# Recurrent retention and a squared-ReLU feed-forward on one core: the second token block's output product done as seven half-size products, with another order around it

## The chip, the core and the metric

The kernel runs on one core of a Trainium2 chip. The core has engines that work side by side, each through its own queue, strictly in order: TensorE (PE in the profile; its weight loads are PEld) for matrix products, VectorE (DVE), ScalarE (ACT), GpSimd (POOL), and SyncE (SP), which issues most transfers. Products land in PSUM, eight banks of 2 KB per partition; everything else works on SBUF. Engines wait for one another through semaphores. The metric is device time in microseconds (us); lower is better.

## What is computed

```
state = gamma * state + outer(k_t, v_t);  y_t = scale * q_t @ state     # 4 batches, 8 heads, 768 steps, head size 64
x = y as 3072 tokens x 512
out = relu(x @ w_in)**2 @ w_out                                         # 512 -> 2048 -> 512
```

The recurrence is computed in chunks of 128 tokens: masked scores within a chunk and a running state between chunks, with the decay put into scaled copies of q and k. There are 24 chunks.

## The kernel before

**Blocks.** The 24 chunks are cut into 11 token blocks (BLOCKS): the first has four chunks, the others two. For a block the feed-forward first computes h = relu(x @ w_in) squared (the *first product*, `first_product`, L848: four matmuls for each of 16 slices of 128 hidden features), with ScalarE taking the relu out of PSUM (L857) and the square done on VectorE (L828) or, for a few, on ScalarE (L826). The *second product* multiplies h by w_out.

**Seven products.** For a 256-token block the second product, cut into two by two halves, can be done as seven products of half size instead of eight, with sums of halves of h (s1 to s4, made per block on VectorE), sums of halves of w_out (t1 to t4, `sum_w_out`, made once) and sums of the results (u, v, and the two output tiles). `seven_products` does this for the blocks in SEVEN, which are 2 to 10 (L28); `last_of_first` does it for half of block 0, whose other half is done plainly (`plain(j)`, L1036, eight steps, each of four matmuls of 512 columns and one of 256). Block 1 does the second product plainly: 32 matmuls of 512 columns (L1174). The last of the seven products of a block is kept back (`kept`) and runs in the next block's first product.

**The order.** Everything is put in order by hand. Blocks yield after each piece, a counter n rises by one for each, and `before(n)` runs whatever was `put` at that place. Block 0's pieces end at place 32, block 1's are places 33 to 48, block 2's begin after 48. `attend(m, ...)` places the steps of chunks 4 to 7: scaling q and k, turning q and k on TensorE through the one PSUM bank "tp" (pool `ps_tp`, one buffer; `transpose_q` L408, `transpose_k` L421), copying the turned k into the tile k_bd by two ScalarE instructions (L428), scores into the one bank "st" (L447) with a mask on VectorE (L454), `state` (L475/L486, copied out to s_bd), and `outputs` into the bank "y" (L515, L523, copied to xt on ScalarE, L531). Later chunks (`attend2`) turn q and k by transfers. In `seven_products` the accumulator pa is a tile of that same bank "tp"; pb, pe and pd are of the four-buffer pool "psf".

**Tiles.** The pool "h2" has three buffers of 4096 elements per partition: at the start `spare`, then the two of block 0, then one for each block in turn. s1, s2 and s4 of blocks 2 to 10 are kept in the tiles k_bds[0], k_bds[1] and v_bds[0], which chunks 4 to 7 use before that.

**Transfers.** SyncE issues q, k, v and w_in; GpSimd issues w_out, four parts of 512 KB that are cast on the way (`load_w_out`, L185, places 6, 8, 11, 14). GpSimd also casts v, zeroes the two k_big tiles and makes constants (`pack_constants`). VectorE zeroes the unused halves of seven other tiles (`zero_off_diagonal`, L375, places 35 on). `keep_awake` (L359) issues idle matmuls early on, while the inputs are on their way.

Of the kernel before, what the change touches and what calls it, by code (L numbers as in the profile page):

```python
# [9 lines left out]
FP32 = mybir.dt.float32  # L10
# [4 lines left out]
ALU = mybir.AluOpType  # L15
# [9 lines left out]
PACK_FROM = 8  # L25


SEVEN = range(2, 11)  # L28


@with_exitstack
def kernel(
# [163 lines left out]
        load_w_in(g)  # L196


    lng = const.tile([P, H], FP32)
    for h in range(H):  # L200
        nc.gpsimd.memset(lng[:, h : h + 1], float(np.log(gammas[h])))
# [125 lines left out]
    HN = DM // 2  # L327
    sums = [const.tile([P, NFB // 2, HN], BF16, name=f"w_sum{i}") for i in range(4)]

    def sum_w_out(half):  # L330

        src = w_out_halves[half].rearrange("s (j k) (n c) -> s k n j c", k=2, n=2)
        (b11, b12), (b21, b22) = ([src[:, k, n] for n in range(2)] for k in range(2))
        t1, t2, t3, t4 = (t[:, 4 * half : 4 * half + 4] for t in sums)
        for out, in0, in1 in ((t1, b12, b11), (t2, b22, t1), (t3, b22, b12), (t4, b21, t2)):
            yield nc.vector.tensor_tensor(out=out, in0=in0, in1=in1, op=ALU.subtract)

    def cast_w(kind, g, halves=(0, 1), on="VVSG"):

# [11 lines left out]

    idle_ps = []

    def keep_awake(n, width=4 * C, pool=ps_f, name="psf"):
        if not idle_ps:
            idle_ps.append(pool.tile([P, 4, P], FP32, name=name))
        wide = max(1, width // C)
        for _ in range(n):
            nc.tensor.matmul(  # L359
                idle_ps[0][:, 0:wide, 0 : width // wide],  # L360
                lhsT=ident[:],
                rhs=ident[:, None, 0 : width // wide].to_broadcast([P, wide, width // wide]),
                start=True,
                stop=True,
            )

    def end_awake():
        idle_ps.clear()
# [3 lines left out]
    xts = {}  # L372

    def zero_off_diagonal(t, hh):
        nc.vector.memset(t[halves[hh], :, 1 - hh, :], 0.0)  # L375

    def scale(engine, out, by, table):
        engine.tensor_tensor(  # L378
# [483 lines left out]
    def seven_products(tb):  # L862
# [4 lines left out]
            t.rearrange("s p hh d -> s (p hh d)").rearrange("s (j t) -> s j t", t=C)  # L867
            for t in (k_bds[0], k_bds[1], v_bds[0])
        )
        s3 = a21  # L870
        t1, t2, t3, t4 = sums
        b11, b21, b22 = (
# [108 lines left out]
    def last_of_first():  # L981
# [34 lines left out]
            add(s1[x], a21[x], a22[x])  # L1016
            add(s2[x], s1[x], a11[x], ALU.subtract)

        def last_sums():
            for x in range(2):  # L1020
                add(s3[x], a11[x], a21[x], ALU.subtract)
            for x in range(2):
                add(s4[x], a12[x], s2[x], ALU.subtract)

        def second_products():
            ops = [ps_f.tile([P, DM], FP32, name="psf") for _ in range(2)]
            pa, pe, pd, pb = (
                t[:, n * HN : (n + 1) * HN]
                for t in [ps_f.tile([P, DM], FP32, name="psf") for _ in range(2)]
                for n in range(2)  # L1030
            )
            oa, ob = (opool.tile([P, DM], FP32, name="osb") for _ in range(2))
            a, u, v = (upool.tile([P, HN], FP32, name=f"u{i}") for i in range(3))
            r0 = 2 * C

            def plain(j):  # L1036
                for f in (2 * j, 2 * j + 1):
                    for c, op in enumerate(ops):
                        nc.tensor.matmul(  # L1039
                            op[:],  # L1040
                            lhsT=h_of(0, f)[:, 0, c * C : (c + 1) * C],
                            rhs=w_out_bf[f // FPQ][:, f % FPQ, :],
                            start=(f == 0),
                            stop=(f == NFB - 1),
                        )
# [17 lines left out]
            nc.scalar.activation(a[:], pa, AF.Copy)  # L1063
# [5 lines left out]
            product(pa, a12, b(1, 0), lo, False)  # L1069
            product(pa, a12, b(1, 0), hi, False)  # L1070
            nc.scalar.activation(oa[:, 0:HN], pa, AF.Copy)
            yield
            product(pd, s1, t1, hi)
            yield
            product(pb, s2, t2, hi)
            add(u[:], pb, a[:])
            yield
            product(pe, a22, t4, hi)
            yield
            product(pb, s3, t3, lo, False)  # L1080
            yield
            product(pb, s3, t3, hi, False)
            add(v[:], pb, a[:])
            add(ob[:, HN:DM], pd, v[:])
            add(ob[:, 0:HN], pe, v[:])

            def last_product():
                product(pd, s4, b(1, 1), range(8), False)
                add(oa[:, HN:DM], pd, u[:])
                yield  # L1090
                nc.sync.dma_start(out[r0 + C : r0 + 2 * C], ob[:])
                yield
                nc.sync.dma_start(out[r0 : r0 + C], oa[:])
                yield

            kept.append(last_product())
            yield

        return first_sums, last_sums, second_products

    open_ps = {}

    def first_unit(tb, g, c, parts=(0, 1)):
# [98 lines left out]
    spare = hpool.tile([P, 4096], BF16, name="h2")  # L1202
    keep_awake(7, pool=ps_y, name="y")
    scale_q4(0, 0)
    scale_q4(0, 1)
    transpose_q4(0, 0, *tp)
# [85 lines left out]
    def attend2(m, d, before, q_at, qturn_at, k_at, turn_at, v_at):  # L1292
# [107 lines left out]
```

## Time and profile before

| | us |
|---|---|
| median of 3 runs (lowest, highest) | 204.95 (204.93, 205.1) |
| the profiled execution's own time | 205.18 |
| its span, first to last instruction | 203.0 |
| PE busy in the span | 195.8 (96%) |
| DVE / ACT / POOL busy | 150.0 / 127.5 / 75.4 |

The profiled execution took 2.18 us more than its span, and is 0.23 us over the median. The granted TensorE clock was 0.999 over the span. Times in the profile's views are counted from the span's start. In the timeline view the columns are start, duration, engine, line, what was done, and in brackets how long the engine had been idle before and for what. A matmul's duration there is its way through the array; the distance between starts is what it costs TensorE. In the chain views the columns are start, length, engine, bank and line.

### The profile page before, as it was taken

The numbers are of one execution on the slowest core, as the hardware profiler recorded it, in microseconds if no ns is written. First come the engines' busy times: TensorE is split into PE (matmuls) and PEld (weight loads), VectorE is DVE, ScalarE is ACT, GpSimd is POOL, SyncE is SP. The second block draws the span as 40 slices with busy tenths as digits, with TensorE's granted clock in tenths as the row PEclk, the third lists the DMA queues.
The fourth block names the chain that finished last, engine by engine and source line by source line (L and its number), as shares of the span: only waits on it lengthen the run. The fifth ranks groups of instructions, "written<-read, shape, count | busy, mean of one in ns | idle before, by whom it ended". The sixth has DMA issues, their size and how long they took to land.

```text
span 203.0 us, 5812 instructions
## 1 busy us (share of the span) xinstructions
PE 195.8 (96%) x2351; PEld 163.3 (80%) x2351; DVE 150.0 (74%) x322; ACT 127.5 (63%) x258; POOL 75.4 (37%) x143
## 2 busy tenths in 40 slices
PE   5989999999999999999999999999999999999993
PEld 1558545669975998999999999999899999999883
DVE  3786898898797679677787777777787787485374
ACT  8764873455744676693794784774785775763730
POOL 8683721087220873461722084323382022100000
PEclk9999999999999999999999999999999999999999
DMA  5999999999798798979999479999999856200202
GB/s 167 356 374 397 321 198 196 243 232 251 226 203 200 190 141 131 200 180 251 145 215 197 140 130 187 175 227 199 166 133 195 155 107 53 103 3 0 107 0 105
DMA packets 92250, 36.55 MB, mean 180 GB/s; under 512 B 68544, under 2 KB 88256, under 8 KB 92224
## 3 DMA queue, kind: packets, MB, share of 16 engines
q1 hardware_dynamic: 77312, 32.52, 67.8%
q0 software_dynamic: 14912, 3.67, 19.2%
q8 instruction: 18, 0.29, 0.6%
q14 instruction: 8, 0.07, 0.1%
HBM read 27.26 MB, written 6.29 MB: 165 GB/s over the span
## 4 chain that ended last, share of the span: by engine, by line
PE 93%; DVE 2%; DMA 2%; issue 1%; ACT 1%; DVEq 0%
PE psf L848 42%; PE psf L882 18%; PE tp L882 7%; PE psf L1039 3%; PE psf L1174 3%; PE psf L1006 3%; DMA qn<-in_q_dram 2%; PE y L805 2%; PE st L749 2%; PE y L798 2%; PE c_ps L776 2%; PE c_ps L644 1%; PE y L359 1%; PE y L523 1%; PE st L447 1%
## 5 line engine op out<-in xcount | busy, mean ns | idle before, releaser
L848 PE MATMUL psf<-xt,w_in_bf 128*128 128x256 bf16 (+2 forms) x880 | 92.3, 259 | 0.2 <-issue 0.2
L848 PEld LDWEIGHTS <-w_in_bf 128*128 128x128 bf16 x880 | 71.2, 98 | 11.4 <-issue 0.2
L857 ACT ACTIVATE h<-psf 128x512 bf16<-128x512 f32 x96 | 56.1, 595 | 21.3 <-PE psf L848 19.0
L828 DVE TENSOR_TENSOR h<-h 128x512 bf16<-128x512 bf16 x80 | 33.6, 432 | 21.6 <-ACT h L857 21.2
L727 POOL COPY v_bd<-v 64x512 bf16<-64x512 bf16 x32 | 21.6, 675 | 75.0 <-DVE v L719 70.9
L882 PEld LDWEIGHTS <-h 128*128 128x128 bf16 x288 | 26.5, 98 | 3.0 <-DVE h L828 0.3
L160 POOL DMA_DIRECT2D k_big<-in_k_dram x32 | 21.1, 675 | 0.0
L882 PE MATMUL psf<-w_sum,h 128*128 128x256 bf16 x136 | 19.1, 273 | 0.0
L882 PE MATMUL tp<-w_out_bf,h 128*128 128x256 bf16 x136 | 19.1, 273 | 0.0
L882 PE MATMUL psf<-w_sum,k_bd 128*128 128x256 bf16 x144 | 17.9, 273 | 0.0
L878 DVE TENSOR_TENSOR u<-psf,u 128x256 f32<-128x256 f32 x18 | 7.6, 424 | 11.2 <-PE psf L882 10.8
L882 PEld LDWEIGHTS <-k_bd 128*128 128x128 bf16 x144 | 13.8, 98 | 1.5
L785 ACT ACTIVATE s_bd<-c_ps 64x256 bf16<-64x256 f32 x29 | 10.7, 370 | 6.5 <-PE c_ps L776 6.5
L878 DVE TENSOR_TENSOR osb<-psf,u 128x256 f32<-128x256 f32 x26 | 10.3, 421 | 6.1 <-PE psf L882 5.8
L378 DVE TENSOR_TENSOR qs<-qn,qf 128x512 bf16<-128x512 f32 x20 | 14.2, 713 | 0.0
L786 ACT ACTIVATE s_bd<-c_ps 64x256 bf16<-64x256 f32 x29 | 11.0, 379 | 0.4
L756 DVE TENSOR_TENSOR pt<-st,cmask 128x512 bf16<-128x512 f32 x16 | 11.0, 688 | 0.1
L719 DVE TENSOR_TENSOR v<-stage,kf 128x512 bf16<-128x512 f32 x16 | 11.0, 685 | 0.0
L812 ACT ACTIVATE xt<-y 128x512 bf16<-128x512 f32 x16 | 9.6, 599 | 1.8 <-PE y L805 1.2
L918 ACT ACTIVATE osb<-tp 128x256 f32<-128x256 f32 x8 | 3.1, 385 | 12.2 <-PE tp L882 12.2
L826 ACT ACTIVATE h<-h 128x512 bf16<-128x512 bf16 x16 | 10.1, 630 | 0.5
L878 DVE TENSOR_TENSOR k_bd<-h 128x512 bf16<-128x512 bf16 x18 | 10.1, 559 | 0.3
(149 smaller groups left out, 296.1 us busy)
## 6 DMA issues: line engine op xcount, KB each, us to landing
qn<-in_q_dram SPq DMA_DIRECT2D x12, 512.0 KB, 5.5
out_dram<-osb SPq DMA_DIRECT2D x23, 256.0 KB, 2.6
stage<-in_v_dram SPq DMA_DIRECT2D x32, 96.0 KB, 4.1
stage<-in_moe_w_in_dram SPq DMA_DIRECT2D x4, 512.0 KB, 7.2
stage<-in_moe_w_in_dram SPq DMA_DIRECT2D x2, 1024.0 KB, 8.4
w_out_bf<-in_moe_w_out_dram POOLq DMA_DIRECT2D x4, 512.0 KB, 10.1
kn<-in_k_dram SPq DMA_DIRECT2D x6, 256.0 KB, 6.3
k_big<-in_k_dram POOLq DMA_DIRECT2D x32, 48.0 KB, 3.8
```

Of the source, the lines that this page charges most:

```text
L160: nc.gpsimd.dma_start(t[rows, :, p, hh, :], k[b, 2 * p + hh, (i + 3 * n) * C : (i + 3 * n + 3) * C].rearrange("(w s) d -> s w d", s=64),)
L378: engine.tensor_tensor(out=out, in0=by, in1=table[:, :, None].to_broadcast([P, H, D]), op=ALU.mult)
L719: nc.vector.tensor_tensor(out=v2.rearrange("s (u p) d -> s u p d", u=2), in0=vn, in1=kf2[:, i, :, :, None].to_broadcast([P, 2, NPAIR, D]), ...
L727: nc.gpsimd.tensor_copy(v_bd[rows, :, hh, :], v2[rows])
L756: nc.vector.tensor_tensor(out=pt[:], in0=st[:], in1=cmask2.rearrange("s r t -> s (r t)")[:, None, :].to_broadcast([P, 2 * NPAIR, C // 2]), ...
L785: nc.scalar.activation(s_bd[halves[0], :, 0, :], c[halves[0]], AF.Copy)
L786: nc.scalar.activation(s_bd[halves[1], :, 1, :], c[halves[1]], AF.Copy)
L828: nc.vector.tensor_mul(hv, hv, hv)
L848: nc.tensor.matmul(hp, lhsT=w_in_bf[g][:, cb, fq * 128 : (fq + 1) * 128], rhs=xts[tb][:, cb, cols], start=(cb == 0), stop=(cb == NCB - 1),)
L857: nc.scalar.activation(hv, hp[:], AF.Relu)
L878: nc.vector.tensor_tensor(out=out, in0=in0, in1=in1, op=op)
L882: nc.tensor.matmul(to, lhsT=left[:, j], rhs=right(j) if callable(right) else right[:, j], start=(start and j == 0), stop=(stop and j == NF ...
```

## The change

Block 1 joins SEVEN. Its s1, s2 and s4 go into a further tile of the pool "h2" (`room`), since the tiles used by the later blocks are still taken. One of its relus gets its square on ScalarE. Around it:

- In block 0's second products the order is other: the second halves of s1·t1 and s2·t2 come before a12·b21, and a22·t4 comes last; s3 and s4 are made at places 26 and 27.
- The sums of w_out are made in other parts: the second half in two pieces of t1, t2 and one of t3, t4.
- `attend` has other places for chunks 4, 6 and 7, and chunk 6's state is copied out wholly by ScalarE.
- `pack_constants` moves from places 27 and 34 to 12 and 15, so GpSimd does it ahead of issuing the fourth part of w_out.
- `zero_off_diagonal` is done by GpSimd.
- `spare` is made early, 128 columns of it are zeroed by VectorE, and `keep_awake` multiplies these zeros: four matmuls of 128 columns for each former one of 512, ten groups at first where there were seven. It no longer waits for the identity.
- One cast of v at the start goes from GpSimd to ScalarE.

```diff
-SEVEN = range(2, 11)
+SEVEN = range(1, 11)
...
+    spare = hpool.tile([P, 4096], BF16, name="h2")
+    still = spare[:, 4096 - P : 4096]
+    nc.vector.memset(still, 0.0)
...
-    def sum_w_out(half):
+    def sum_w_out(half, which=range(4), js=slice(0, 4)):
...
-        for out, in0, in1 in ((t1, b12, b11), (t2, b22, t1), (t3, b22, b12), (t4, b21, t2)):
-            yield nc.vector.tensor_tensor(out=out, in0=in0, in1=in1, op=ALU.subtract)
+        made = ((t1, b12, b11), (t2, b22, t1), (t3, b22, b12), (t4, b21, t2))
+        for out, in0, in1 in (made[n] for n in which):
+            nc.vector.tensor_tensor(out=out, in0=in0, in1=in1, op=ALU.subtract)
...
-            idle_ps.append(pool.tile([P, 4, P], FP32, name=name))
-        wide = max(1, width // C)
-        for _ in range(n):
...
+            idle_ps.append(pool.tile([P, P], FP32, name=name))
+        for _ in range(4 * n):
+            nc.tensor.matmul(idle_ps[0][:], lhsT=still, rhs=still, start=True, stop=True)
...
-        nc.vector.memset(t[halves[hh], :, 1 - hh, :], 0.0)
+        nc.gpsimd.memset(t[halves[hh], :, 1 - hh, :], 0.0)
...
+        if tb == 1:
+            room = hpool.tile([P, 4096], BF16, name="h2").rearrange("e (n j t) -> e n j t", n=4, t=C)
+            s1, s2, s4 = (room[:, n] for n in range(3))
...
+            product(pd, s1, t1, hi)
+            product(pb, s2, t2, hi)
+            add(u[:], pb, a[:])
+            yield
             product(pa, a12, b(1, 0), lo, False)
+            yield
             product(pa, a12, b(1, 0), hi, False)
             nc.scalar.activation(oa[:, 0:HN], pa, AF.Copy)
-            yield
-            product(pd, s1, t1, hi)
-            yield
-            product(pb, s2, t2, hi)
-            add(u[:], pb, a[:])
-            yield
-            product(pe, a22, t4, hi)
             yield
             product(pb, s3, t3, lo, False)
             yield
             product(pb, s3, t3, hi, False)
             add(v[:], pb, a[:])
             add(ob[:, HN:DM], pd, v[:])
+            yield
+            product(pe, a22, t4, hi)
             add(ob[:, 0:HN], pe, v[:])
...
-            relu(h_of(tb, g * FPQ, (g + 1) * FPQ)[:, :, cols], open_ps.pop((tb, g, c)))
+            relu(h_of(tb, g * FPQ, (g + 1) * FPQ)[:, :, cols], open_ps.pop((tb, g, c)), (tb, c, g) == (1, 1, 2))
...
-            put(22, last_sums)
+            put(26, last_sums[0])
+            put(27, last_sums[1])
...
-    keep_awake(7, pool=ps_y, name="y")
+    keep_awake(10, pool=ps_y, name="y")
...
-    cast_pair_v(2, 1)
+    cast_pair_v(2, 1, on_scalar=True)
...
-            put(scaled + 2 if m == 4 else scaled, scale_q, m, 1)
+            put(scaled + 2, scale_q, m, 1)
...
-        put(18 if m == 4 else places[0], scale_kv, m)
+        put(16 if m == 4 else places[0], scale_kv, m)
...
-        put(places[3], state, m)
+        put(places[3], state, m, 2 if m == 6 else 1)
...
-    for half, at_places in enumerate(((20, 20, 20, 20), (24, 24, 26, 26))):
-        made = sum_w_out(half)
-        for place in at_places:
-            put(place, next, made)
-    attend(4, 13, (19, 21, 23, 25, 29))
+    put(20, sum_w_out, 0)
+    put(22, sum_w_out, 1, (0, 1), slice(0, 2))
+    put(24, sum_w_out, 1, (0, 1), slice(2, 4))
+    put(26, sum_w_out, 1, (2, 3))
+    attend(4, 12, (17, 19, 21, 23, 28))
     attend(5, None, (25, 28, 30, 32, 34))
-    attend(6, 31, (33, 35, 37, 39, 42))
-    attend(7, None, (38, 42, 44, 46, 49))
+    attend(6, 29, (33, 35, 37, 39, 42))
+    attend(7, None, (36, 40, 43, 45, 48))
     packed = pack_constants()
-    put(27, next, packed)
-    put(34, next, packed)
+    put(12, next, packed)
+    put(15, next, packed)
```

More of the change, by code (lines that the diff above doesn't have):

```diff
@@ L328 @@
     sums = [const.tile([P, NFB // 2, HN], BF16, name=f"w_sum{i}") for i in range(4)]
-    def sum_w_out(half):
+    def sum_w_out(half, which=range(4), js=slice(0, 4)):
         src = w_out_halves[half].rearrange("s (j k) (n c) -> s k n j c", k=2, n=2)
-        (b11, b12), (b21, b22) = ([src[:, k, n] for n in range(2)] for k in range(2))
-        t1, t2, t3, t4 = (t[:, 4 * half : 4 * half + 4] for t in sums)
-        for out, in0, in1 in ((t1, b12, b11), (t2, b22, t1), (t3, b22, b12), (t4, b21, t2)):
-            yield nc.vector.tensor_tensor(out=out, in0=in0, in1=in1, op=ALU.subtract)
+        (b11, b12), (b21, b22) = ([src[:, k, n, js] for n in range(2)] for k in range(2))
+        t1, t2, t3, t4 = (t[:, 4 * half : 4 * half + 4][:, js] for t in sums)
+        made = ((t1, b12, b11), (t2, b22, t1), (t3, b22, b12), (t4, b21, t2))
+        for out, in0, in1 in (made[n] for n in which):
+            nc.vector.tensor_tensor(out=out, in0=in0, in1=in1, op=ALU.subtract)
     def cast_w(kind, g, halves=(0, 1), on="VVSG"):
@@ L352, with keep_awake @@
     idle_ps = []
-    def keep_awake(n, width=4 * C, pool=ps_f, name="psf"):
+    def keep_awake(n, pool=ps_f, name="psf"):
         if not idle_ps:
-            idle_ps.append(pool.tile([P, 4, P], FP32, name=name))
-        wide = max(1, width // C)
-        for _ in range(n):
[L359 to L365, printed above, removed]
+            idle_ps.append(pool.tile([P, P], FP32, name=name))
+        for _ in range(4 * n):
+            nc.tensor.matmul(idle_ps[0][:], lhsT=still, rhs=still, start=True, stop=True)
     def end_awake():
@@ L1017, in first_sums, with third_sums, fourth_sums @@
             add(s2[x], s1[x], a11[x], ALU.subtract)
-        def last_sums():
+        def third_sums():
             for x in range(2):
                 add(s3[x], a11[x], a21[x], ALU.subtract)
+        def fourth_sums():
             for x in range(2):
@@ L1068, in second_products @@
             yield
-            product(pa, a12, b(1, 0), lo, False)
-            product(pa, a12, b(1, 0), hi, False)
-            nc.scalar.activation(oa[:, 0:HN], pa, AF.Copy)
-            yield
             product(pd, s1, t1, hi)
-            yield
             product(pb, s2, t2, hi)
@@ L1077, in second_products @@
             yield
-            product(pe, a22, t4, hi)
+            product(pa, a12, b(1, 0), lo, False)
+            yield
+            product(pa, a12, b(1, 0), hi, False)
+            nc.scalar.activation(oa[:, 0:HN], pa, AF.Copy)
             yield
@@ L1097, in second_products @@
             yield
-        return first_sums, last_sums, second_products
+        return first_sums, (third_sums, fourth_sums), second_products
     open_ps = {}
@@ L1200, in small_pt @@
         return ptpool.tile([P, NPAIR, 2, C], BF16, name="pt").rearrange("s p hh t -> s (p hh t)")
-    spare = hpool.tile([P, 4096], BF16, name="h2")
-    keep_awake(7, pool=ps_y, name="y")
+    keep_awake(10, pool=ps_y, name="y")
     scale_q4(0, 0)
```

## The prediction

> **What bounds the kernel now.** I read the page's busy times and its chain first, then the chain in order of time from 39 to 44 and from 56 to 68 us, where the change works, and there the timelines of PE and ACT and the landing times of the w_out transfers.
>
> ```profile
> PE 195.8 (96%) x2351; PEld 163.3 (80%) x2351; DVE 150.0 (74%) x322; ACT 127.5 (63%) x258; POOL 75.4 (37%) x143
> ...
> PE 93%; DVE 2%; DMA 2%; issue 1%; ACT 1%; DVEq 0%
> ...
> L826 ACT ACTIVATE h<-h 128x512 bf16<-128x512 bf16 x16 | 10.1, 630 | 0.5
> ```
>
> PE is 93% of the chain: a matmul less is time less, and a wait of PE is time more. Two waits lie in block 0:
>
> ```profile
> 39.56 0.60 PE L1006 MATMUL psf<-w_sum,h 128*128 128x256 bf16 x4
> 40.14 0.59 PE L1039 MATMUL psf<-w_out_bf,h 128*128 128x512 bf16 x2
> ```
> ```profile
> L185 POOL DMA_DIRECT2D w_out_bf<-in_moe_w_out_dram x2: 742/746/750, 25.0 to 25.8; - x2
> ...
> DMA to landing us min/median/max: 10.9/12.6/14.3
> ```
> ```profile
> 42.42 0.27 PE L1006 MATMUL psf<-w_out_bf,h 128*128 128x256 bf16 x1
> 42.73 0.39 ACT L1063 ACTIVATE u<-psf 128x256 f32<-128x256 f32 x1 [0.60 <-PE psf L1006]
> 43.17 0.38 PE L1006 MATMUL psf<-w_out_bf,h 128*128 128x256 bf16 x2 [0.47 <-ACT u L1063]
> ```
>
> Four matmuls of 256 columns cost 0.44, so plain(6) could start at 40.00; it starts at 40.14, just after the fourth part of w_out lands (25.8 + 14.3 = 40.1). At 42.42 + 0.11 = 42.53 PE is free and waits 0.64 for ScalarE's copy of pa. Block 1:
>
> ```profile
> 56.71 0.25 PE c_ps L486 x8
> 56.95 1.00 PE psf L848 x16
> 57.95 1.73 PE psf L1174 x8
> 59.68 0.22 PE y L523 x4
> 59.90 0.03 issue
> 59.93 0.38 PE y L523 x4
> 60.32 0.22 PE tp L421 x4
> ```
> ```profile
> 56.52 0.60 ACT L857 ACTIVATE h<-psf 128x512 bf16<-128x512 f32 x1 [0.30 <-PE psf L848]
> 57.02 0.36 ACT L498 ACTIVATE s_bd<-c_ps 64x256 bf16<-64x256 f32 x1
> 57.99 0.60 ACT L857 ACTIVATE h<-psf 128x512 bf16<-128x512 f32 x1 [0.61 <-PE psf L848]
> 60.35 0.60 ACT L531 ACTIVATE xt<-y 128x512 bf16<-128x512 f32 x1 [1.77 <-PE y L523]
> 60.85 1.19 ACT L428 ACTIVATE k_bd<-tp 64x512 bf16<-64x512 bf16 x2
> ```
> ```profile
> 79.42 0.88 PE tp L882 x8
> ```
>
> The plain product is gapless (eight matmuls in 1.73, 0.216 each); those of 256 columns take 0.109. The last piece of block 1's first product ends, by the timeline's starts, at 57.79; call that E. ScalarE takes each piece out just behind PE, and needs 1.19 to 1.21 for the two copies of a turned k.
>
> **The change part by part.**
>
> *Fewer matmuls.* Block 1 drops 32 x 0.216 = 6.91 and gets 56 x 0.109 = 6.10: **-0.81**, all on PE. Eight of the 56 run within block 2's first product. VectorE gets four sums of 512 (0.42), two of 1024 (0.68) and five adds out of PSUM (0.42), about 5.1 us, and loses ten memsets (two of 0.17, eight of 0.27, 2.5 us). It is busy 3.86 and 3.36 of 4 us in 56 to 64 but 1.81 in 64 to 68; I cost this at nothing because of the next item, under which it catches up; without that cover PE would wait some 0.5 for the last square before the last two a22·t4.
>
> *A new wait on the bank "tp".* In the new order the four turns of chunk 7's k (place 40) stand right behind E, and right behind them the first matmul of pa, which is a tile of the same one-buffer pool. It must wait until both k_bd copies have read the bank. In front of these on ScalarE now stand the relu of the third piece, both halves of chunk 6's state (one was VectorE's), the square moved to ScalarE, and the relu of the fourth piece. From the rows' starts: relu at 56.52; s_bd 0.50 later, 57.02; the second s_bd 0.39 later (70.40 to 70.79 for the same pair), 57.41; the square 0.40 later, 57.81; the relu 0.54 later (a square's 0.63 less the overlap of about 0.1 that ScalarE's rows show), 58.35; k_bd 0.50 later, 58.85, for 1.20: 60.05. With 0.05 for the signal pa starts at 60.10; PE has been free since 57.79 + 0.22 = 58.01. The wait is 2.09. Bounds: without square and second s_bd in front (relu at 57.99 as now) 1.73; with k_bd ahead even of that relu 1.44; with no overlap between ScalarE's instructions 2.35. I take **+2.0**. Behind pa in PE's queue stands everything else: a22·t4, chunk 6's outputs, the scores of chunk 7, then block 2; nothing of it can pass, so the end moves by all of it.
>
> *Block 0's order.* The wait of 0.64 for the copy of pa goes: 0.87 of matmuls now lie between. Chunk 4's second scores and state (0.45) move ahead of plain(6); they fill its wait for w_out and push it only if PE gains nothing before. New is a wait of chunk 5's scores: the turn of its k now stands right behind chunk 4's outputs, with 0.88 of matmuls (1.55 before) until the scores that need k_bd. From plain(6) at 40.14: two plain steps 1.95, four products 0.87, pa 0.44, outputs 0.67, turn 0.22 give 44.29, and the scores' place at 45.17. ScalarE takes the outputs (from 44.27) and only then k_bd, 44.77 to 45.97; scores at 46.02, waiting 0.85 (0.5 if k_bd went first, 1.2 if ScalarE overlaps nothing). The work from plain(6) to block 1's first matmul was 47.63 - 40.14 = 7.49; less 0.45, 0.64 and the old 0.07 wait of scores, plus 0.85 and 0.08, it is 7.26: **-0.23**. VectorE's u stands late too (its in-order sums end near 45.3), inside the same 0.85.
>
> *Chunk 6's q* is scaled at 29 and 31, its second half perhaps late for the turn at 33: **+0.07**, 0 to 0.3. *The old wait* at 59.9 (eight matmuls of 0.055 in 0.63) goes with chunk 6's mask ready long before: **-0.15**, -0.2 to 0.
>
> *Start.* Idle matmuls start near 0.95 (first engine instructions at 0.74, the memset about 0.1) instead of 2.19, end near 5.2 if each 128 columns still cost 0.107, before the first turn at 5.47. A gain is bounded by the k transfer that VectorE's scaling at 9.62 could have had at 9.1: 0 to 0.5. It ends at plain(6), where w_out lands at 40.1. **0** if PE is at least 0.3 early there, +0.30 if not early at all. In this trace idle matmuls cost 0.427 until 8.17 and then half. [...]
>
> *GpSimd's queue.* The constants (memsets 0.42, iota 0.59, 0.16, 0.53: 1.70) now stand ahead of issuing w_out's fourth part. Its landing stays at 40.1 if it waits behind the third part (landing 25.0 + 10.9 = 35.9, so long after the new issue near 27.5); it is 41.8 if landing follows issue. 0 to +1.7; I take 0, as the parts land one after another. Ten memsets (eight of 0.52 as L315's, two of about 0.3, 4.8 us) follow chunk 7's v at about 52; behind them wait casts and transfers for chunks from 8 on, and GpSimd had 9.4 us idle before 66.42, so 0. A cast of GpSimd slows VectorE: a sum of 0.68 beside it took 1.07 (41.08); sums beside its k_big memsets took 0.68 (43.90, 44.50). *v's cast* on ScalarE ends near 16.3, used at 16.45; 0, at most 0.1. SyncE issues the same bytes, one store later by a place or two.
>
> **Sum.** -0.81 + 2.0 - 0.23 + 0.07 - 0.15 = +0.88. The profiled 205.18 becomes 206.06; the median shown was 0.23 lower: **205.8**.
>
> **Rivals.** Measurement here tells 0.2% (0.41 us) from no change.
> - *The bank is free early, faster.* Without the wait the sum is -1.12, 203.8. It is faster by 0.41 only if the wait is under 0.71, that is, k_bd read out by 58.67; the floor by rows is 1.44. Against it speak the single buffer and the order. Some 204.3, chance 0.10, mostly for what I have not seen.
> - *The low ends meet:* wait 1.44 to 1.6, block 0 at -0.5: 205.0 to 205.3, no change. 0.14.
> - *w_out lands late:* +1.7 at plain(6), 207.5. 0.07.
> - *Memsets on GpSimd slow VectorE.* At the cast's rate (0.39 per 0.62) 4.8 us of them would cost VectorE 3.0, of which the wait on "tp" hides about 2: 206.8. The two rows at 43.90 and 44.50 speak against it. 0.07. [...]
> - *The forecast,* 205.4 to 206.4: 0.62.
>
> Slower 0.76, same 0.14, faster 0.10. The range goes from both low ends nearly met, 205.0, to the high wait and no early start (+0.35, +0.35, +0.3), **205.0 to 206.8**.
>
> **What would show it.** PE idle of about 2 us at the first pa of block 1, waiting on ScalarE's k_bd; none at the copy of pa in block 0; about 0.85 at chunk 5's first scores; 8 x 0.109 more in block 2's first product; plain(6) right after the w_out landing near 40. Wrong if ScalarE reads the bank within a microsecond of the turn, or w_out's fourth part lands well off 40.

## The result and the profile after

The changed kernel took **206.07 us** (median of 13 runs, 205.16 to 207.73) beside 204.81 for the kernel before (13 runs, 204.2 to 205.1): a ratio of **1.0085** (95%: 1.0065 to 1.0106), slower by 0.6 to 1.1%. The prediction was 205.8, with slower at 0.76. The profiled execution took 205.68, its span was 203.9.

The 13 times fall into two groups by the clock that was granted to TensorE: seven at 1.000 with a median of 205.83, six at 0.992 with a median of 207.47. None of the 89 runs of the kernel before that stand beside the experiments lies under 0.997. At a full clock the change costs 205.83 - 204.81 = 1.02, 0.5%; what lies behind the second group is told in the last section.

First the page of the changed kernel: busy times, shares of the chain, and the group of matmuls that write the bank "tp".

```profile
PE 195.6 (96%) x2429; PEld 168.9 (83%) x2432; DVE 151.9 (75%) x324; ACT 128.7 (63%) x261; POOL 81.0 (40%) x152
...
PE 80%; DMA 6%; DVE 3%; SPq 3%; ACT 2%; POOL 2%; issue 2%; DVEq 0%; ACTq 0%
...
L883 PE MATMUL tp<-w_out_bf,h 128*128 128x256 bf16 x152 | 21.5, 273 | 2.0 <-ACT k_bd L426 2.0
```

PE is as busy as before, but its share of the chain fell from 93% to 80%. Little of that is time lost: for long stretches the chain now follows other engines while PE is at work, some 3.5 points more at the start, where it goes through a transfer of v and comes to PE at 15.50, and some 7 in block 2. But in two places PE has to stand still. The last line names one: one wait of 2.0 for ScalarE's copies of k_bd. The chain there, in order of time (start, length, what):

```profile
55.77 0.60 ACT h L855
56.37 0.26 ACT s_bd L496
...
57.04 0.44 ACT h L824
...
57.70 0.60 ACT h L855
58.30 0.47 ACT k_bd L426
...
58.78 0.60 ACT k_bd L426
...
59.42 0.82 PE tp L883 x6
```

This is ScalarE's queue as the prediction had it: relu of the third unit, the state's two copies (the second is left out), the square, relu of the fourth unit, two copies of k_bd, and only then pa. From the starts of the matmuls, PE stood still for 2.16 here (57.26 to 59.42).

The second place is one that the prediction did not have. It is the chain that ends in the scores of chunk 10, in block 2:

```profile
73.50 0.61 DVE v L717
...
74.16 0.26 POOL v_bd L725
...
76.30 0.91 POOL ks_bdp L708
...
77.97 5.37 DMA kT<-ks_bdp
...
83.39 0.41 PE st L747 x8
```

VectorE scales chunk 9's v late, GpSimd's casts of that v wait for it, the cast of chunk 10's k stands behind them in GpSimd's queue, and the transfer that turns this k lands 0.47 after PE wanted it. The kernel before had no wait there. Its lines for the same scaling and the same cast:

```profile
72.18 0.68 DVE L719 TENSOR_TENSOR v<-stage,kf 128x512 bf16<-128x512 f32 x1
```
```profile
75.11 1.39 POOL L710 CAST ks_bdp<-stage 64x512 bf16<-64x512 f32 x2
```

There the transfer was issued at 76.53 and landed at 80.53; PE took the k at 82.46. So the issue is 1.44 later now (77.97), and the transfer itself takes 5.37 instead of 4.00. PE wanted it at 82.92. By these numbers either delay alone would not have made PE wait: 77.97 + 4.00 = 81.97, and 76.53 + 5.37 = 81.90.

**Where the time went, from the starts of matmuls in the two profiled executions.**

| stretch | before | after | difference |
|---|---|---|---|
| to the first matmul of 512 columns of block 0's first product | 21.59 | 20.69 | -0.89 |
| from there to block 1's first matmul | 26.05 | 26.07 | +0.02 |
| block 1's first product | 10.10 | 10.23 | +0.12 |
| from its end to block 2 (chunk 7's outputs included in both) | 9.29 | 9.59 | +0.30 |
| block 2 to the last matmul | 132.57 | 133.96 | +1.39 |

The sum is +0.94, the spans differ by 0.95. The first two rows cut elsewhere than the prediction did: plain(6) began at 40.14 before and at 39.55 after, and from there to block 1's first matmul it was 7.49 before and is 7.21 now. The +0.30 is 6.91 - 5.23 = 1.68 of matmuls saved, 2.16 of new wait, and the old wait at 59.9 (0.20) gone. The +1.39 is the last product kept back from block 1 (8 x 0.109 = 0.87) and the 0.47, all but 0.05 of it.

What lies around the span changed too: 2.23 in the median of the runs of the kernel before, 1.76 in those of the kernel after. So of the 0.95 only 0.50 is left between the two profiled times, while the medians at a full clock differ by 1.02, as the profiled execution of the kernel before was a long one of its kind (spans from 201.9 to 203.2).

### The profile page after: what moved, and what is told of

Read it like the earlier page. It is cut to its first block, busy times and chain, and to the rows that moved or that the text cites. A ratio compares the mean times of both kernels' runs of the same rounds, so it can differ in the third digit from the quotient of the medians.

```text
span 203.9 us, 5987 instructions
## 1 busy us (share of the span) xinstructions
PE 195.6 (96%) x2429; PEld 168.9 (83%) x2432; DVE 151.9 (75%) x324; ACT 128.7 (63%) x261; POOL 81.0 (40%) x152
## 4 chain that ended last, share of the span: by engine, by line
PE 80%; DMA 6%; DVE 3%; SPq 3%; ACT 2%; POOL 2%; issue 2%; DVEq 0%; ACTq 0%
PE psf L846 37%; PE psf L883 18%; PE tp L883 7%; DMA vn<-in_v_dram 4%; PE psf L1042 3%; PE psf L1007 3%; DMA kT<-ks_bdp 3%; SPq L115 2%; PE st L747 2%; PE y L803 2%; PE y L796 1%; PE c_ps L774 1%; ACT k_bd L426 1%; SPq L179 1%; PE y L521 1%
## 5 line engine op out<-in xcount | busy, mean ns | idle before, releaser
L826 DVE TENSOR_TENSOR h<-h 128x512 bf16<-128x512 bf16 x79 | 34.7, 452 | 19.2 <-ACT h L855 18.8
L883 PEld LDWEIGHTS <-h 128*128 128x128 bf16 x344 | 31.7, 98 | 5.6 <-issue 1.9
L883 PE MATMUL tp<-w_out_bf,h 128*128 128x256 bf16 x152 | 21.5, 273 | 2.0 <-ACT k_bd L426 2.0
L883 PE MATMUL psf<-w_sum,h 128*128 128x256 bf16 x168 | 23.4, 273 | 0.0
L879 DVE TENSOR_TENSOR u<-psf,u 128x256 f32<-128x256 f32 x20 | 8.5, 423 | 11.6 <-PE psf L883 11.2
L879 DVE TENSOR_TENSOR osb<-psf,u 128x256 f32<-128x256 f32 x29 | 11.5, 421 | 6.7 <-PE psf L883 6.3
L824 ACT ACTIVATE h<-h 128x512 bf16<-128x512 bf16 x17 | 10.7, 630 | 0.5
```

Source lines behind the costliest of these rows:

```text
L826: nc.vector.tensor_mul(hv, hv, hv)
L879: nc.vector.tensor_tensor(out=out, in0=in0, in1=in1, op=op)
L883: nc.tensor.matmul(to, lhsT=left[:, j], rhs=right(j) if callable(right) else right[:, j], start=(start and j == 0), stop=(stop and j == NF ...
```

## The experiments

All but the eighth start from the kernel after the change; each ratio is to runs of the kernel before on the same chip.

### 1. The bank free early

```diff
-    attend(7, None, (36, 40, 43, 45, 48))
+    attend(7, None, (36, 38, 43, 45, 48))
```

> Chunk 7's k is turned two units of block 1's first product earlier (place 38 instead of 40), so that the bank tp is read out before the first matmul of pa asks for it; all else is as after the change. Bank theory: the wait of 2.16 at 57.2 goes. Next to be late is the square of the third unit on ScalarE (it ended at 57.5, the fifth matmul of pa wants it near 57.5) and the square of the fourth (relu to 58.3, square to 58.8, wanted near 58.5): 0.3 to 0.6 of waiting stays. So 1.5 to 1.9 are gained over the run of 205.7 that was profiled: 203.8 to 204.2. Gate theory (the five of thirteen times near 207.4, whose mean granted clock is 0.992 instead of 1.000, come from the clock falling to half for about 3.4 us because of this wait): all times lie together at a clock of 1.000. Rival, a cause at the start of the kernel: the two groups of times stay, 1.7 apart. Rival, the wait only moves to the next thing in the block: less than 0.5 gained, 205.2 or more.

Measured: 204.49 (12 runs, 204.12 to 205.44), ratio 0.9991 (0.9975 to 1.0006); all clocks at 0.998 or more. The wait of 2.16 is gone. The two that were expected next are there, 0.20 and 0.63, the second for the square of the fourth unit:

```profile
57.72 0.63 ACT h L824
...
58.37 0.61 ACT h L855
...
59.00 0.44 DVE h L826
...
59.48 0.39 PE psf L883 x2
```

The wait for chunk 10's k grew to 0.69: its transfer was issued at 76.52, as in the kernel before, but took 5.59, and PE was there earlier. Against the times at a full clock, 205.83, the turn alone is worth 1.34, less than the 1.5 to 1.9 expected. The bank theory holds, and the group at 0.992 went with the wait. (Six of the thirteen were at 0.992, not five as the text above has it.)

### 2. The old start

```diff
-            nc.tensor.matmul(idle_ps[0][:], lhsT=still, rhs=still, start=True, stop=True)
...
+                lhsT=ident[:],
...
-    keep_awake(10, pool=ps_y, name="y")
...
+    keep_awake(7, pool=ps_y, name="y")
```

> Only the idle matmuls at the start are as before the change (on the identity, 512 columns each, in fewer instructions, the first after the identity is built). The prediction's step: an earlier start is worth nothing, since plain(6) waits for w_out near 40 either way: within 0.3 of after the change at equal clock, PE about 0.9 later at 31, no wait or a smaller one at plain(6). Rival, the start is worth its whole 0.9: 0.6 to 0.9 slower than after the change. Gate theory: some of the times still are about 1.7 above the others, with a mean granted clock of 0.992, as the wait on the bank tp is still there. Rival, the start makes them: all at 0.999 to 1.000.

Measured: 207.21 (4 runs, 207.08 to 207.32), ratio 1.0113 (1.0091 to 1.0136). That is 1.38 more than after the change at a full clock, where the prediction's step allowed 0.3. The wide matmuls begin at 21.59 again, the wait on "tp" stands at 58.05 instead of 57.20, and a wait for a turned k in block 2 (chunk 9's here) grew to 1.26. Taking off the 0.79 that this one grew by, the start itself is worth about 0.6. The fourth part of w_out was issued at 27.7 and landed 12.4 later, at 40.1 again. All four clocks were at 0.999 or 1.000 in spite of the wait of 2.17; four runs are too few to say more.

### 3. Block 1 plain

```diff
-SEVEN = range(1, 11)
+SEVEN = range(2, 11)
...
-            relu(h_of(tb, g * FPQ, (g + 1) * FPQ)[:, :, cols], open_ps.pop((tb, g, c)), (tb, c, g) == (1, 1, 2))
+            relu(h_of(tb, g * FPQ, (g + 1) * FPQ)[:, :, cols], open_ps.pop((tb, g, c)))
```

> Block 1's second product is the plain one again (64 matmuls of 512 columns); start, order in block 0, GpSimd's zeroing and the places of the turns stay as after the change. Bank theory with the prediction's terms: the seven products themselves give -0.81, the wait costs +2.16, so without both the run of 205.7 becomes 204.3 (204.0 to 204.6), about 0.5 under the kernel before; all at a granted clock of 1.000. Also the wait of 0.47 at 82.8 goes if VectorE's additional sums in block 2 are what delays chunk 9's turned k; then 203.9. Rival, the other parts of the change cost what is lost: 205 or more.

Measured: **203.80** (10 runs, 203.67 to 204.61), ratio 0.996 (0.9941 to 0.9978): faster than the kernel before. Block 1's plain product is 32 matmuls of 512 columns (the 64 expected above count block 0's too). Neither the wait on "tp" nor the one for chunk 10's k is there. So the other parts of the change gain 1.0, and doing block 1 by seven products as it is placed here loses 2.0 at a full clock. A plain second product begins with the first chunk's tokens, so it needs the last squares late; the seven products need the second chunk's h almost at once.

### 4. Chunk 9's k cast early

```diff
-        8: (37, 41, 44, 46, 48), 9: (0, 0, 49, 51, 53), 10: (50, 54, 55, 57, 60), 11: (0, 0, 60, 63, 68)
+        8: (37, 41, 44, 46, 48), 9: (0, 0, 47, 51, 53), 10: (50, 54, 55, 57, 60), 11: (0, 0, 60, 63, 68)
```

> GpSimd casts chunk 9's k two places earlier (place 47 instead of 49), ahead of chunk 8's v, which waits for VectorE; all else is as after the change. If the wait of 0.47 at 82.8 comes from this queue: it goes, 0.3 to 0.5 faster at equal clock, the turn of that k issued earlier. If the transfer itself sets it (it took 5.4), nothing changes, or the wait moves to another chunk. The two groups of times, 1.7 apart, stay in any case, as the wait on the bank tp is still there.

Measured: 206.31 (11 runs, 204.99 to 208.14), 205.80 at a full clock; the wait stayed, 0.53. This was the wrong k: the chain shown above ends in chunk 10's. But that k's transfer was issued 0.9 earlier here (77.04) and still landed late, as it took 6.42: the issue alone does not make the wait. Four of the eleven were at 0.992.

### 5. The wait made longer

```diff
-                nc.scalar.activation(s_bd[head, :, hh, :], of, AF.Copy)
+                for _ in range(4 if m == 6 and hh else 1):
+                    nc.scalar.activation(s_bd[head, :, hh, :], of, AF.Copy)
```

> The kernel after the change, with the second copy of chunk 6's state on ScalarE made four times instead of once, all ahead of the two k_bd copies that the bank tp waits for: three more of 0.39, so the wait at 57.2 grows from 2.16 to 3.3. Bank theory alone: 1.2 slower than after the change at equal clock (its times at a clock of 1.000 have a median of 205.9), 207.1, and still two groups. Gate theory: the longer the wait, the more often the clock falls; most or all of the times at a granted clock of about 0.992 and near 208.8, and the profile then shows half the clock for one stretch of 3.4 right behind the wait, 256 columns taking 0.213 there instead of 0.109. Rival, the groups have nothing to do with the wait: no more of them at 0.992 than the 10 of 24 so far, and no half clock behind the wait.

Measured: 209.58 (4 runs, 208.47 to 210.31), ratio 1.0236 (1.0204 to 1.0269). The wait is 3.40. All four runs lost clock: two at 0.992 and two at 0.984, which is what one and two stretches of 3.413 at half clock would make of a span of 208 (an estimate from the length in experiment 6). In the profiled one, at 0.992, the clock was at half from 60.66 to 64.06, and the six matmuls of 256 columns behind the wait took 1.44 instead of 0.82.

### 6. Chunk 10's k ahead of chunk 9's v, too early

```diff
-        8: (37, 41, 44, 46, 48), 9: (0, 0, 49, 51, 53), 10: (50, 54, 55, 57, 60), 11: (0, 0, 60, 63, 68)
+        8: (37, 41, 44, 46, 48), 9: (0, 0, 49, 51, 53), 10: (50, 54, 52, 55, 60), 11: (0, 0, 60, 63, 68)
```

> The kernel after the change, with GpSimd's cast of chunk 10's k queued ahead of the casts of chunk 9's v (place 52 instead of 55) and its turn issued at 55 instead of 57. Theory of the queue: that cast stood behind the v casts, which wait for VectorE's scaling, which block 1's additional sums have pushed back by about 1; ahead of them it starts at 73.4, right after the state of chunk 8 is taken, not at 76.3; the transfer lands near 81 instead of 83.3, the wait of 0.47 at 82.8 goes: 0.4 to 0.5 faster at equal clock. Rival, the transfer is slow because the DMA engines are busy (it takes 5.4): it lands later than 5.4 after its issue and the wait stays. Rival: a wait for chunk 9's outputs or a transfer issued behind takes its place, no gain. The wait at 57.2 stays 2.16, and some times stay near 1.7 above the others.

At place 52 the cast comes ahead of chunk 8's last use of the same tile (the second part of its state, place 54), so in this kernel and the next that state is made from chunk 10's k, and PE has to wait for the cast. Measured: 207.02 (4 runs, 206.16 to 207.87). The wait at 82.8 is gone; the 1.24 at 74.7 that took its place is this edit's own. As a test of the queue it settles little: the transfer was issued at 77.05, not much earlier than the 77.97 after the change, and took 4.11, and PE came for the k 1.24 later.

Its profiled execution was one of those at 0.992, and its wait on "tp" is the same 2.16 at 57.18 as after the change, so it shows what the clock did. By stretches of one us: start and end, length, busy times of PE, PEld, DVE, ACT and POOL, granted clock, DMA share, GB/s:

```profile
58.00:59.00 1.00, 0.00 (x0) 0.00 (x0) 0.96 (x3) 0.99 (x3) 0.48 (x1) 1.00 0.80 184
59.00:60.00 1.00, 0.60 (x6) 0.54 (x6) 0.93 (x4) 0.35 (x1) 0.00 (x0) 0.98 1.44 207
60.00:61.00 1.00, 1.00 (x7) 0.69 (x6) 0.63 (x2) 0.00 (x0) 0.00 (x0) 0.50 1.04 227
...
62.00:63.00 1.00, 1.00 (x10) 0.88 (x8) 0.00 (x0) 0.38 (x1) 0.00 (x0) 0.50 0.76 215
63.00:64.00 1.00, 1.00 (x11) 0.88 (x9) 0.00 (x0) 0.60 (x1) 0.00 (x0) 0.82 1.34 296
64.00:65.00 1.00, 1.00 (x13) 0.91 (x12) 0.45 (x1) 0.00 (x0) 0.00 (x0) 1.00 1.16 210
```

PE is at work again from 59.4, but from just before 60 the clock is 0.50 until 63.4, and then full again. By the clock records of the trace it is 3.413 at half, after 54.613 at full, which is 16 times 3.413. Half a clock for 3.413 costs up to 1.71; the two groups of this kernel lie 1.67 apart (206.18 and 207.86).

### 7. Both waits, first attempt

```diff
+            first_sums(slice(0 if tb == 1 else 4, 8))
...
+            if tb == 1:
+                product(pa[:], a11, b11, range(8), True, True)
+                nc.scalar.activation(a[:], pa[:], AF.Copy)
+                yield
+                product(pe[:], a22, t4, range(8), True, True)
+                yield
...
-    attend(6, 29, (33, 35, 37, 39, 42))
-    attend(7, None, (36, 40, 43, 45, 48))
+    attend(6, 29, (33, 35, 37, 39, 41))
+    attend(7, None, (35, 37, 43, 45, 48))
...
+        8: (37, 41, 44, 46, 48), 9: (0, 0, 49, 51, 53), 10: (50, 54, 52, 55, 60), 11: (0, 0, 60, 63, 68)
```

> Both waits taken out together, seven products kept: chunk 7's k scaled at 35 and turned at 37; block 1's second product begins with all eight matmuls of pa, which need only the first chunk's h, then chunk 6's outputs, then a22 times t4; the first sums of block 1 stand behind the last square on VectorE; chunk 10's k is cast as in the run before this one. Theory: 204.49 (the turn alone moved by two) less the 0.83 that waited for the squares of the third and fourth units and less the 0.69 that waited for chunk 10's k: 203.0 (202.8 to 203.4), under the 203.8 with the plain product in block 1, by about the 0.81 that the seven products save; all at a granted clock of 1.000. Rival, the waits move on to the next late thing in VectorE's queue (chunk 9's v, the mask of chunk 7): 203.6 to 204.4, no better than the plain product.

Measured: 204.43 (12 runs, 204.38 to 205.46), ratio 0.9989 (0.9976 to 1.0002). It carries the wait of 1.24 from the edit before, and one of 0.45 at 60.3 for the first sums, which VectorE now made behind the last square although it had stood idle for 1.1 ahead of it. Both were made by these edits, so nothing is decided here. The wait on "tp" is gone.

### 8. The new start alone, on the kernel before

```diff
+    still = spare[:, 4096 - P : 4096]
+    nc.vector.memset(still, 0.0)
...
-    keep_awake(7, pool=ps_y, name="y")
+    keep_awake(10, pool=ps_y, name="y")
```

> The kernel before, with the idle matmuls at the start as after the change (on zeros that VectorE writes, 128 columns each, forty instead of seven of 512 ahead of the first turn), and nothing else changed. The prediction's step: worth 0 (at most 0.3), because plain(6) waits for the fourth part of w_out near 40.1 whenever PE gets there: 204.5 to 204.8. Rival: the loads move forward with the start and w_out lands earlier too, near 39.4, as it does after the change: the start is worth 0.7 to 0.9, 203.9 to 204.1.

Measured: 204.33 (12 runs, 204.17 to 204.86), ratio 0.9988 (0.9976 to 1.0001): 0.5 faster, between the two expectations. The chain around plain(6), which begins with the second of these lines:

```profile
39.08 0.44 PE psf L1003 x4
39.51 0.86 PE psf L1036 x4
```

There is no gap: PE came 0.5 earlier and found its weights. The landing had moved along: here the last part of w_out was issued at 25.3 and took 13.8, so it landed at 39.1, where before it was 40.1. In the kernel after the change it was issued at 28.1 and took 11.3. First the view of this kernel, then that of the kernel after the change:

```profile
L185 POOL DMA_DIRECT2D w_out_bf<-in_moe_w_out_dram x4: 742/756/962, 22.1 to 25.3; - x4
...
DMA to landing us min/median/max: 6.9/10.3/13.8
```

```profile
L185 POOL DMA_DIRECT2D w_out_bf<-in_moe_w_out_dram x4: 740/772/959, 22.2 to 28.1; - x4
...
DMA to landing us min/median/max: 7.0/10.1/11.3
```

That is 39.4; plain(6) started at 39.55 there, without a gap before it. Of the earlier start about 0.4 was lost again in this eighth kernel at 15.4, where PE waited for the second of two casts of v by GpSimd; the change gives that cast to ScalarE, and 0.32 of waiting for the first is left.

### 9. Chunk 10's k behind the state

```diff
-    attend(7, None, (36, 40, 43, 45, 48))
+    attend(7, None, (36, 38, 43, 45, 48))
...
-        8: (37, 41, 44, 46, 48), 9: (0, 0, 49, 51, 53), 10: (50, 54, 55, 57, 60), 11: (0, 0, 60, 63, 68)
+        8: (37, 41, 44, 46, 48), 9: (0, 0, 49, 51, 55), 10: (50, 54, 54, 55, 60), 11: (0, 0, 60, 63, 68)
```

> The turn of chunk 7's k at 38 (as in the first experiment, 204.49, with a wait of 0.69 left at 81.4), and chunk 10's k cast right behind chunk 8's last state (place 54 instead of 55, its turn issued at 55 instead of 57), with chunk 9's v scaled and cast behind it (55 instead of 53). Theory of the queue: the cast of chunk 10's k no longer waits behind v casts that wait for VectorE; its transfer is issued near 73.5 instead of 76.5 and lands before 80; the wait of 0.69 goes and nothing takes its place: 203.8 (203.7 to 204.0). Rival, the transfer itself is slow among the others: it stays, 204.3 to 204.6. Rival, chunk 9's v or a state comes late instead: 204.2 or more with PE waiting in 74 to 81.

Measured: 204.39 (12 runs, 204.2 to 205.74), ratio 0.9987 (0.9967 to 1.0008). The wait for chunk 10's k is gone, and the last of the rivals came true: a wait of 0.57 at 77.5, for a square that stands on VectorE behind the scaling of chunk 9's v, now two places later. The gain is 0.1. The transfer took 3.82. (The profiled executions here and in experiment 7 are long ones, 205.74 and 205.46: PE waited 1.66 and 1.14 at 7.35 for a scaled q, which the other traces do not show.)

### 10. Both waits

Block 1's order and the places of chunks 6 and 7 from experiment 7, those of chunks 9 and 10 from experiment 9; the first sums are left where the change has them.

> Both waits taken out with the seven products kept: chunk 7's k scaled at 35 and turned at 37; block 1's second product begins with all eight matmuls of pa, which need only the first chunk's h, then chunk 6's outputs, then a22 times t4; chunk 10's k cast as in the run before this one; the first sums stay where the change has them. Theory: 204.49 less 0.83 (the two waits for squares at 58.1 and 58.7 in the first experiment) less 0.69 (the wait for chunk 10's k): 203.0 (202.8 to 203.3), 0.8 under the plain product in block 1 (203.80), which is what the fewer matmuls are worth, and at a clock of 0.997 or more. Rival, VectorE is now the bound of block 1 and the waits move on: 203.6 or more, no better than the plain product.

Measured: **203.42** (12 runs, 203.34 to 205.75), ratio 0.9952 (0.9925 to 0.998). The chain where block 1's second product begins, and the place of the 0.57 that is left:

```profile
57.24 0.87 PE tp L883 x8
58.11 0.45 PE y L521 x8
58.56 1.53 PE psf L883 x14
```
```profile
72.07 1.03 DVE v L717
73.10 0.75 DVE h L826
...
75.35 0.35 DVE h L826
```

Block 1 runs without a gap: pa, chunk 6's outputs, a22·t4 follow one another. In block 2 VectorE scales chunk 9's v (1.03 beside GpSimd's cast, 0.68 in the kernel before) ahead of the squares, and PE waits 0.57 for the last of these. So the time lies 0.1 above the range expected. The seven products no longer lose 2.0 against the plain one (203.80): by the medians they now gain 0.38, by the two profiled spans 0.33. But the intervals of the two ratios overlap (0.9941 to 0.9978 there), so that gain is not shown. One run, 205.75 at a clock of 0.991, stands alone; what lowered the clock there was not seen.

### 11. ScalarE's queue shorter

```diff
-        put(places[3], state, m, 2 if m == 6 else 1)
+        put(places[3], state, m)
...
-            relu(h_of(tb, g * FPQ, (g + 1) * FPQ)[:, :, cols], open_ps.pop((tb, g, c)), (tb, c, g) == (1, 1, 2))
+            relu(h_of(tb, g * FPQ, (g + 1) * FPQ)[:, :, cols], open_ps.pop((tb, g, c)))
```

> The kernel after the change with the square of block 1's third unit and the second half of chunk 6's state on VectorE again, so that ScalarE has two operations less ahead of the k_bd copies. The prediction's bounds say a wait of 1.44 to 1.73 instead of 2.16: taken 1.6, so 0.5 to 0.6 faster at equal clock (205.3 against 205.9), if VectorE's two more operations (0.42 each) hide under the wait. Rival, VectorE is then late with the squares for the sixth matmul of pa and a22 times t4: less than 0.3 gained. Gate theory: with 1.6 of a window of 3.4 idle instead of 2.16, fewer of the times have a granted clock of 0.992 than the 10 of 24 with the longer wait; rival, as many.

Measured: 205.48 (12 runs, 204.81 to 206.02), ratio 1.0028 (1.0008 to 1.0049). The wait is 1.72 from the starts of matmuls, which the profile's waits put at:

```profile
PE tp L883 <- ACT k_bd L426: 1.6, 1, 1.6
```

The prediction's bound for this queue was 1.73. The gain at a full clock, 0.35, less than the 0.5 to 0.6 expected, is about the 0.44 of the wait less a wait for chunk 10's k that is 0.14 longer. All twelve clocks were at 0.998 or more.

### 12. The scaling early, the casts late

To the edits of experiment 10 this one is added:

```diff
+    def cast_v2(m):
...
-        put(v_at, scale_v2, m)
+        put(53 if m == 9 else v_at, scale_v2, m)
+        put(v_at, cast_v2, m)
```

> As the run with both waits taken out (203.42), but VectorE scales chunk 9's v at place 53 again, as after the change, and only GpSimd's casts of it stay behind its cast of chunk 10's k (55). The wait of 0.57 left at 75.1 there was for the last square of block 2, which stood on VectorE behind that scaling (1.03 long beside GpSimd's cast, 0.69 without). Theory: the wait goes, as both queues now have the early thing first: 202.85 (202.7 to 203.0). Rival, VectorE's work in block 2 is too much wherever the scaling stands: it waits somewhere else in 70 to 83, 203.2 or more.

Measured: **203.12** (6 runs, 203.1 to 203.66), ratio 0.9932 (0.9915 to 0.995), the fastest of all and 0.7% under the kernel before. The time lies between the two expectations. The wait fell from 0.57 to 0.41 only: by the chain, squares and sums still kept VectorE at work without a pause from 73.10 to 75.60, where they had from 73.10 to 75.70 in experiment 10. That VectorE's work in block 2 is too much, as the rival has it, fits this but is not shown; what takes the rest away was not tried. The interval of the ratio overlaps that of experiment 10.

## Why the prediction was right, and where it was not

The verdict and its cause were right. The time came out right partly because terms that were wrong cancelled.

- **The new wait on the bank "tp"**, taken as +2.0 (2.09 worked out): 2.16. Right in place, cause and size. Experiment 11 took away what the lower bound of 1.73 left out, and measured 1.72; experiment 1 took away the wait.
- **Fewer matmuls**, -0.81: as counted, -1.68 in block 1 and +0.87 in block 2.
- **The old wait at 59.9**, -0.15: -0.20. **Chunk 6's q**, +0.07: block 1's first product is 0.12 longer, 0.11 of it at the turn of this q.
- **Block 0's order**, -0.23: -0.28, from plain(6) to block 1's first matmul (7.49 before, 7.21 after). The parts were right too: no wait for the copy of pa; 0.29 of waiting for VectorE's u and 0.50 at chunk 5's scores, where 0.85 was predicted for both. (The table's +0.02 also holds the 0.45 of chunk 4's scores and state, which now stand ahead of plain(6), less the 0.14 that PE had waited there.)
- **Start**, 0: this is the step that failed. It held the landing of w_out at 40.1 and so the start of plain(6) at 40.14, whatever else starts earlier. Measured, plain(6) started at 39.55, 0.59 earlier. The loads moved with the start: w_out landed at 39.4 after the change and at 39.1 with the new start alone (experiment 8), but at 40.1 with the old start and all else changed (experiment 2). Experiments 8 and 2 put the start at 0.5 and 0.6. The 0 also counted on an earlier full clock, which no trace had shown when it was written; measured, the full clock was granted from 4.38 on after the change, from 8.15 on before, and from 8.08 on with the old start (experiment 2).
- **Additional sums on VectorE**, costed at nothing because VectorE catches up under the wait on "tp": also wrong. It did not catch up by block 2: in 70 to 76 it was busy for 5.91 of 6 us, where it had been for 4.74. Its late scaling of chunk 9's v went through GpSimd's queue into a transfer and came out as 0.47 of PE. In experiment 3, without these sums and the rest of the seven products, the wait is not there; in 9, with another order in GpSimd's queue, it goes too. This is one half of the wait. The other is that the transfer took 5.37 instead of 4.00; why is open. In the traces without a wait for this k (before, experiments 2, 3, 6 to 10 and 12) it took 3.8 to 4.8, in those with one (after, 1, 4, 5, 11) 5.4 to 6.4.
- **The time around the span** was taken as unchanged; it fell by 0.47. Neither the start (2.22 in experiment 8) nor block 1's products (1.80 in experiment 3) explain it. Its cause is open.

So between the two profiled executions -0.6 of start and -0.5 around the span were missed on one side, +0.5 in block 2 and +0.16 of the wait on "tp" on the other, and they differ by 0.50, not by 0.88. In six of thirteen runs +1.6 of lost clock comes on top. That 205.8 is nearly the median at a full clock, 205.83, is luck: the profiled execution before was 0.37 above its median of 13, the one after 0.15 below the median at a full clock.

Of the rivals, "the bank is free early" did not happen by itself, but experiment 1 made it happen. It gave 204.49, near the "some 204.3" put down for that rival, by other terms: the start helped, and the squares were late next (0.83). "The low ends meet" fell, as the wait was above the forecast and not at 1.44 to 1.6. "w_out lands late" went the other way. "Memsets on GpSimd slow VectorE" fell: from 51.9 to 56.3 GpSimd zeroed tiles, and VectorE's squares beside it took 0.42 and its scalings 0.69, as ever. Behind it GpSimd cast chunk 9's k (56.38 for 1.50), and the square at 56.57 took 0.83. So here too VectorE was slower beside GpSimd's cast and not beside its zeroing, as in the trace before (a sum of w_out took 1.07 beside the cast, 0.68 beside the zeroing).

## What to carry to other kernels

Before work is put into a bank that another step still holds, write down the other engine's queue up to the instruction that frees the bank: here ScalarE's operations in front of two copies, and the copies, made PE wait 2.16, more than the 1.68 of matmuls that block 1 saved, and a turn two places earlier took the wait away (experiment 1). An operation that is cheap on an engine with time to spare can still be late for the next queue behind it, as the scaling of chunk 9's v was here (0.61 at the head of a chain that made PE wait 0.47); follow it until it reaches the bound engine. And do not hold a transfer's landing fixed when the work ahead of it moves: w_out's moved from 40.1 to 39.1 with the new start alone.

## What the runs showed that was not expected

**Behind a wait of 2.16 us the clock was at half for 3.4 us in some of the runs.** With PE idle for 2.16, 10 of 24 runs (the kernel after the change and experiment 4) had a mean clock of 0.992; with the same wait in experiments 2 and 6 it was 2 of 8. With 3.40 idle, 4 of 4 had 0.992 or 0.984; with 1.72, none of 12. Half a clock for 3.413 in a span of 206 makes a mean of 1 - 0.5 x 3.413 / 206 = 0.992, and the stretch itself was seen in the traces of experiments 5 and 6.

The clock records of six traces fit that the place of the wait decides. In the traces of this case, every stretch of full clock is a whole number of times 3.413 long (57 times before, 59 after, from 42 to 59 in all, besides the 16 above), so a grid of such stretches can be laid from the moment at which the full clock begins. That moment differs from execution to execution, and with it the part of the wait that falls into one stretch:

| trace | full clock from | the wait | most of it in one stretch | half clock behind it |
|---|---|---|---|---|
| after | 4.38 | 57.26 to 59.42 | 1.73 | no |
| experiment 4 | 4.01 | 57.34 to 59.51 | 1.27 | no |
| experiment 2 | 8.08 | 58.10 to 60.26 | 1.18 | no |
| experiment 11 | 6.76 | 57.20 to 58.92 | 0.95 | no |
| experiment 6 | 5.34 | 57.24 to 59.40 | 2.16 | yes |
| experiment 5 | 6.04 | 57.57 to 60.97 | 3.08 | yes |

So in these traces the clock fell to half at the end of a stretch of which 2.16 or more was idle (63%), and did not where 1.73 was (51%). By this grid, as an estimate, an idle time of 2.16 lies wholly within one stretch in (3.413 - 2.16) / 3.413 = 37% of all positions that the grid can have; 12 of the 32 runs lost clock. One of 1.72 would do so in 50%, and never halved the clock in twelve runs. Two things this leaves open: an idle time of 3.40 cannot put more than 1.73 into each of two stretches, so the two runs at 0.984 need something further; and the one run at 0.991 in experiment 10 belongs to a kernel whose trace has no such wait.

The cost was 1.6 to 1.7 in the runs that it hit: there a wait of 2.16 cost 3.8, in 12 runs of 32. The kernel before, with 0.64 as its longest wait in the middle, never paid it in its 89 runs here.
